# Attention with an RMS norm on q and k, then a token mixer and an MLP: batch 0's first loads, warming products, the cast of V and four fillers are rearranged

## The chip, the cores and the metric

The kernel runs on one core of one Trainium2 chip. The metric is the device time of one execution, in microseconds (us). Four runs of the kernel before gave 580.72, 579.29, 584.65 and 579.07; their median is 580.01. The engines are called PE (TensorE), DVE (VectorE), ACT (ScalarE), POOL (GpSimd) and SP (SyncE, which here only issues transfers).

## The reference

```
q, k, v: (8 batches, 12 heads, 448 tokens, 64), float32
q_n = rmsnorm(q, g_q);  k_n = rmsnorm(k, g_k)         # over the 64
attn = softmax(q_n k_n^T / 8);  o = attn v
x = o, heads side by side: (8, 448, 768)
u = x + (U V applied along the 448 tokens)            # rank 32
out = u + relu(u w_ch1) w_ch2                         # 768 -> 3072 -> 768
```

## The kernel before

**Tiles and stages.** A batch's 12 heads are three groups t of four heads, and each group is two pairs p of two heads. The 448 tokens lie as 112 partitions by 4. For a group, `load` and `load_v` fetch k, q and v (L187, L201); `squares` and `reduce` (L217, L227) give sums of squares, `rsqrt` (L234) makes two ScalarE instructions of them (Ln and Exp). For a pair, `scale` (L239) multiplies k and then q by the norm on DVE, from two SBUF inputs; `transposes` (L250) turns the eight pieces on PE and takes them out of PSUM with a multiply by the gain `gg` for q (L258) and a copy for k (L259). `scores` and `expo` (L267, L277) make exponentials of 112 x 896, `values` (L281) multiplies them with v and divides. Then the mixing with U and V and the MLP follow. From batch 1 on, attention is woven into the MLP of the batch before by weights (`weave`), so PE always has dense matmuls at hand.

**The head.** Batch 0 has no MLP to hide in. `head` (L591) writes its order by hand: loads first, then set-up, warming products, and the norm of group 0 in halves (A: heads 0 and 1, Bh: heads 2 and 3), then 24 slots. Slot n runs exponential n, then the pieces that `at(n, ...)` put on it in the order of writing, then the scores n + 2. After the slots, mixing and the first MLP columns (`first`, L724) follow, and the dense loop `mlp` (L482).

**Fillers and warming.** `heat(n)` (L755) issues n products of 128 x 512 on a zeroed tile into a PSUM buffer; nobody reads it. Its buffer is one of three of the pool `ps_mm` (tag "mm"), which `transposes`, `setup_u`, the mixing steps and every second `values` of batch 0 also take in turn; a new user waits until the one three before it has been read out. `heat(NWARM)` (L604) runs ahead of the first gain product.

**Queues.** Each engine executes its instructions in the order of writing. SP issues the loads of the head one after another: k and q of group 0 in halves (k, q, k, q), then groups 1 and 2, U and V, v of groups 0 to 2, group 3 (L594 to L602). ScalarE's queue issues only the two small gain loads (L135), after it has loaded its table (L121). POOL does squares of group 1's k and of groups 2 and 3, the casts of v (`cast_v`, L212), the two partial copies of V (L156, L157) and issues the weight loads. `yield_port` (L718) makes POOL wait for a scaling on DVE.

**The parts that the change touches.** `setup_v` (L154) casts V from float32 to bf16 in another order of its columns and makes two shifted copies; it stands in slot 11. `gain` (L137) multiplies the product of the two gains (formed at L607) with a one on PE and copies it to `gg`; its copy L141 stands on DVE ahead of the evacuation of the first transposes. The loads' line is

```
nc.sync.dma_start(qks[t, s][:, h:h + n], (k, q)[s][b, h0 + h:h0 + h + n]...)   # L198
```

Of the kernel before, what the change touches and what calls it, by code (L numbers as in the profile page):

```python
# [12 lines left out]
AF = mybir.ActivationFunctionType  # L13
# [4 lines left out]
def kernel(  # L18
# [13 lines left out]
    nc = tc.nc  # L32
# [7 lines left out]
    NJ = 4  # L40
# [43 lines left out]
    V4 = consts.tile([P, S], BF16, name="V4")  # L84
    Vsh = consts.tile([P, 2, P], BF16, name="Vsh")
    gg = consts.tile([P, 1], FP32, name="gg")
    grow = consts.tile([1, 2, 2, D], FP32, name="grow")
    one = consts.tile([1, 1], FP32, name="one")
    eps = consts.tile([SP, 1], FP32, name="eps")
    NWARM, NH = 16, 2  # L90
    FA, FM, NPE, FA0 = (0.74, 0.77), 0.09, 14, 0.66
    flat = Tw.rearrange("p f c n -> p (f c n)")
    lent = [0]
# [1 line left out]
    def lend(p, shape, dtype):  # L95

        n = 1
        for d in shape:
            n *= d
        n *= 2 if dtype == FP32 else 1  # L100
        a = flat[0:p, lent[0]:lent[0] + n]
        lent[0] += (n + 15) // 16 * 16
        a = a.bitcast(FP32) if dtype == FP32 else a
        names = "abcd"[:len(shape)]
        return a if len(shape) == 1 else a.rearrange(
            f"p ({' '.join(names)}) -> p {' '.join(names)}", **dict(zip(names, shape)))
# [30 lines left out]
    def gain():  # L137

        pg = ps_mm.tile([P, 1], FP32, tag="mm")
        nc.tensor.matmul(pg, grow[:, 0].rearrange("o a d -> o (a d)"), one, start=True, stop=True)  # L140
        nc.vector.tensor_copy(gg, pg)  # L141
# [4 lines left out]
    Vf = lend(P, [S], FP32)  # L146
# [3 lines left out]
    def load_mix():  # L150
        nc.sync.dma_start(Uf, moe_U.rearrange("(p j) r -> p (j r)", j=NJ))
        nc.sync.dma_start(Vf, moe_V.rearrange("r s -> () r s").to_broadcast([4, rank, S]))

    def setup_v():  # L154
        nc.scalar.activation(V4.rearrange("r (j p) -> r j p", j=NJ), Vf.rearrange("r (p j) -> r j p", j=NJ), AF.Copy)
        nc.gpsimd.tensor_copy(Vsh[:, 0, 0:64], V4[:, 384:448])  # L156
        nc.gpsimd.tensor_copy(Vsh[:, 1, 64:128], V4[:, 0:64])  # L157

# [26 lines left out]
    qks, vts, sqs, rstds, qkns, qkTs, scs, x3_of = {}, {}, {}, {}, {}, {}, {}, {}  # L185

    def load(t, parts=1, ss=(0, 1)):  # L187
        b, h0, n = t // 3, (t % 3) * HG, HG // parts
        for s in ss:
            if t in (2, 3):  # L190
                qks[t, s] = spare[0:SP, t - 2, s]
            elif (t, s) in ((1, 1), (5, 1)):
                qks[t, s] = k1
            else:
                qks[t, s] = loads.tile([SP, HG, NJ * D], FP32, tag="qk", name="qk", bufs=3)
        for h in range(0, HG, n):
            for s in ss:
                nc.sync.dma_start(qks[t, s][:, h:h + n],  # L198
                                  (k, q)[s][b, h0 + h:h0 + h + n].rearrange("h (p j) d -> p h (j d)", j=NJ))

    def load_v(t):  # L201
# [25 lines left out]
    def reduce(t, hs=ALL, ss=(0, 1)):  # L227
        if t not in rstds:
            rstds[t] = norm.tile([SP, 2, HG, NJ], FP32, tag="rstd", name="rstd", bufs=3)
        for s in ss:  # L230
            nc.vector.tensor_reduce(rstds[t][:, s, hs].rearrange("p h j -> p (h j)"),  # L231
                                    sqs[t, s][:, hs].rearrange("p h (j d) -> p (h j) d", d=D), AX, OP.add)
# [6 lines left out]
    def scale(t, pr):  # L239
        rstd, qkn = rstds[t], norm.tile([SP, 2, NJ, 2, D], BF16, tag="qkn", name="qkn")  # L240
        qkns[2 * t + pr] = qkn
        hp = slice(2 * pr, 2 * pr + 2)
        for s in range(2):
            nc.vector.tensor_tensor(  # L244
                qkn[:, s].rearrange("p j h d -> p h j d"),
                qks[t, s][:, hp].rearrange("p h (j d) -> p h j d", d=D),
                rstd[:, s, hp].rearrange("p h j -> p h j ()").to_broadcast([SP, 2, NJ, D]),
                OP.mult)

    def transposes(p):  # L250
        qkn = qkns[p].rearrange("p s j h d -> p (s j) (h d)")
        qkT = attn.tile([P, 2, S], BF16, tag="qkT")
        qkTs[p] = qkT
        if p < NPE:
            pt = ps_mm.tile([P, 2, S], BF16, tag="mm")
            for i in range(2 * NJ):
                nc.tensor.transpose(pt.rearrange("d s (j p) -> d (s j) p", j=NJ)[:, i, :], qkn[:, i, :], ident[:SP, :SP])  # L257
            nc.vector.tensor_scalar(qkT[:, 1], pt[:, 1], gg, None, OP.mult)  # L258
            nc.vector.tensor_copy(qkT[:, 0], pt[:, 0])  # L259
        else:  # L260
            nc.sync.dma_start_transpose(qkT.rearrange("d s (j p) -> d (s j) p", j=NJ), qkn)

# [253 lines left out]
    def attention(b, extra={}):  # L516
# [14 lines left out]
        for p in range(b * 6, b * 6 + 6):  # L531
# [5 lines left out]
            if p + 1 < NP and (p + 1 >= NPE or not odd):  # L537
                add(.5, transposes, p + 1)
# [52 lines left out]
    def head():  # L591

        A, Bh = slice(0, 2), slice(2, 4)
        load(0, 2)  # L594
        load(1)
        load(2)
        load_mix()
        load_v(0)
        load_v(1)
        load_v(2)  # L600
        load(3)
        load_v(3)  # L602
        setup()
        heat(NWARM)  # L604
        squares(0, A)
        reduce(0, A)
        nc.vector.tensor_mul(grow[:, 0], grow[:, 0], grow[:, 1])  # L607
        squares(0, Bh, (0,))
        rsqrt(0, A)
        squares(0, Bh, (1,))  # L610
        reduce(0, Bh, (0,))
        scale(0, 0)
        gain()
        reduce(0, Bh, (1,))
        transposes(0)
        heat(3)
        squares(1, ALL, (0,), nc.gpsimd)
        rsqrt(0, Bh)
        scores(0, (0, 1))
        fill = {n: [] for n in range(24)}  # L620

        def at(n, fn, *args):
            fill[n].append(lambda: fn(*args))

        at(0, scale, 0, 1)
        at(0, reduce, 1, ALL, (0,))
        at(0, heat, 3)
        at(0, transposes, 1)
        at(1, heat, 3)
        at(1, squares, 1, ALL, (1,))  # L630
        at(1, reduce, 1, ALL, (1,))
        at(1, yield_port, 0, 1)
        at(1, squares, 2)
        at(1, load_w1, 0)
        at(2, heat, 2)
        at(3, rsqrt, 1)
        at(3, scale, 1, 0)
        at(3, yield_port, 1, 0)
        at(3, nc.gpsimd.tensor_copy, Uc, Uf)
        at(3, cast_v, 0)  # L640
        at(3, heat, NH)
        at(4, heat, 2)
        at(5, heat, 1)
        at(6, heat, 1)
        at(5, transposes, 2)
        at(5, scale, 1, 1)
        at(5, yield_port, 1, 1)
        at(6, cast_v, 1)
        at(6, load_w1, 1)
        at(7, setup_u, 0)  # L650
        at(7, reduce, 2, ALL, (0,))
        at(8, transposes, 3)
        at(8, reduce, 2, ALL, (1,))
        at(8, cast_v, 2)
        at(9, setup_u, 1)
        at(9, heat, 1)
        at(10, values, 0, 0)
        at(11, values, 0, 1)
        at(11, setup_v)
        at(11, rsqrt, 2)  # L660
        at(11, scale, 2, 0)
        at(12, mix_a, 0, 0)
        at(12, heat, 1)
        at(13, transposes, 4)
        at(13, scale, 2, 1)
        at(13, load, 4)
        at(13, load_v, 4)
        at(13, load_w1, 2)
        at(14, values, 1, 0)
        at(14, yield_port, 2, 1)  # L670
        at(14, squares, 3)
        at(15, values, 1, 1)
        at(16, transposes, 5)
        at(16, load, 5)
        at(16, load_v, 5)
        at(16, load_w1, 3)
        at(16, cast_v, 3)
        at(16, mix_b, 0, 0)
        at(17, values, 2, 0)
        at(18, values, 2, 1)  # L680
        at(18, mix_a, 0, 1)
        at(19, values, 3, 0)
        at(19, mix_b, 0, 1)
        at(20, values, 3, 1)
        at(20, mix_a, 0, 2)
        at(21, values, 4, 0)
        at(21, mix_b, 0, 2)
        at(22, values, 4, 1)
        at(22, mix_a, 0, 3)
        at(23, mix_b, 0, 3)  # L690
        at(23, mix_a, 0, 4)
        for n in range(24):
            expo(*divmod(n, 4))
            for piece in fill[n]:
                piece()
            if n + 2 < 24:
                scores((n + 2) // 4, ((n + 2) % 4,))
        first(0, range(0, 3), True)
        values(5, 0)
        values(5, 1)  # L700
        mix_b(0, 4)
        first(0, (3,), False)
        first(1, range(0, 4), True)
        mix_a(0, 5)
        first(0, (4,), False)
        first(1, (4,), False)
        mix_b(0, 5)
        reduce(3)
        rsqrt(3)
        first(0, (5,), False)  # L710
        first(1, (5,), False)
        scale(3, 0)
        scale(3, 1)
        squares(4, ALL, (0,))
# [91 lines left out]
```

## Time and profile before

| | us |
|---|---|
| median of four runs | 580.01 (579.07 to 584.65) |
| the profiled execution's own time | 581.62 |
| its span, first to last instruction | 579.8 |
| PE busy in it | 563.0 (97%) |
| DVE, ACT, POOL busy | 398.0, 280.1, 79.1 |
| first product on PE | 3.81 |
| first scores (L273) | 11.23 |
| last exponential of batch 0 (L278) ends | 40.20 |
| first column product of the MLP (L732) | 41.46 |

Times in a profile are counted from the first instruction of the span. In a timeline a line gives the start, the duration of the group, the engine, the line of the kernel, the operation with what it writes and reads, how many instructions of the kind stand together, and in brackets how long the engine had been idle and what released it. In a table of stretches, each engine has its busy time and the number of its instructions; then follow the mean granted PE clock (1.00 is full), the mean busy share of the 16 DMA engines and the rate.

### The profile page before, as it was taken

What the parts mean: (1) busy time and instruction counts of PE and PEld (TensorE: products, weight loads), DVE (VectorE), ACT (ScalarE), POOL (GpSimd) and SP (SyncE); (2) the same over time, 40 slices, a digit from 0 to 9 for tenths busy, and PEclk for the clock granted to TensorE, in tenths of its full rate; (3) what the DMA queues carried; (4) which work ended last, traced back from release to release, by engine and by line L of the source; (5) the groups of instructions that cost most, each with busy time, mean ns of one, the idle gap of its engine ahead of it and who ended that gap; (6) DMA issues with size and microseconds to landing.
All of it is one profiled execution on the core that took longest, in us unless ns stands there. A gap on an engine that the chain in (4) does not pass through costs nothing.

```text
span 579.8 us, 11362 instructions
## 1 busy us (share of the span) xinstructions
PE 563.0 (97%) x4613; PEld 306.5 (53%) x4613; DVE 398.0 (69%) x811; ACT 280.1 (48%) x413; POOL 79.1 (14%) x122
## 2 busy tenths in 40 slices
PE   6899999999999999999999999999999999999997
PEld 2365556544465555544456555544456555554464
DVE  5868987399975787747777498756767587453342
ACT  5855663167621876166651677236661386302200
POOL 4742421000020001000020001000002010000010
PEclk9999999999999999999999999999999999999999
DMA  9999998514463355635536354646245431040021
GB/s 208 242 239 237 218 176 169 120 47 98 112 167 85 84 125 118 150 87 112 128 82 130 83 129 112 152 112 125 62 86 162 100 97 33 29 110 0 1 55 54
DMA packets 103648, 67.22 MB, mean 116 GB/s; under 512 B 54716, under 2 KB 102060, under 8 KB 103596
## 3 DMA queue, kind: packets, MB, share of 16 engines
q1 hardware_dynamic: 93988, 56.77, 41.8%
q0 software_dynamic: 9376, 9.44, 9.9%
q8 instruction: 36, 0.59, 0.4%
q10 hardware_dynamic: 232, 0.30, 0.2%
q14 instruction: 16, 0.13, 0.1%
HBM read 52.19 MB, written 11.01 MB: 109 GB/s over the span
## 4 chain that ended last, share of the span: by engine, by line
PE 85%; DVE 8%; DMA 3%; ACT 1%; issue 1%; POOL 1%; DVEq 0%; POOLq 0%; ACTq 0%
PE ph L488 35%; PE pb L413 10%; PE o L299 7%; PE pe L413 7%; PE po L413 7%; PE sc L273 7%; PE pa L413 6%; DMA qkT<-qkn 2%; DVE qkn L244 2%; PE pu L337 2%; DVE rstd L231 1%; ACT E L278 1%; PE warm L759 1%; PE first L732 1%; PE pt L257 1%
## 5 line engine op out<-in xcount | busy, mean ns | idle before, releaser
L488 PE MATMUL ph<-u,w1b 128*128 128x512 bf16 (+1 forms) x1128 | 232.9, 354 | 0.3
L278 ACT ACTIVATE E<-sc 112x896 bf16<-112x896 f32 x184 | 159.9, 914 | 59.8 <-PE sc L273 58.2
L488 PEld LDWEIGHTS <-w1b 128*128 128x128 bf16 x1128 | 102.8, 98 | 108.6 <-issue 22.4
L413 PEld LDWEIGHTS <-hT 128*128 128x128 bf16 x1080 | 101.2, 98 | 71.5 <-issue 8.8
L491 ACT ACTIVATE hT<-ph 128x384 bf16<-128x384 f32 (+1 forms) x95 | 51.4, 543 | 136.2 <-PE ph L488 134.4
L493 DVE TENSOR_SCALAR hT<-ph 128x512 bf16<-128x512 f32 (+1 forms) x93 | 57.9, 622 | 53.2 <-PE ph L488 52.4
L299 PEld LDWEIGHTS <-E 112*128 112x128 bf16 x1472 | 59.2, 99 | 16.5 <-DVE xs L306 1.9
L299 PE MATMUL o<-va,E 112*128 112x65 bf16 x1440 | 61.8, 195 | 0.8 <-DVE xs L306 0.8
L244 DVE TENSOR_TENSOR qkn<-qk,rstd 112x512 bf16<-112x512 f32 x84 | 56.9, 715 | 7.8 <-ACT rstd L237 3.9
L273 PE MATMUL sc<-qkT 64*128 64x448 bf16 x384 | 56.1, 358 | 3.1 <-ACT E L278 1.1
L720 POOL COPY scratch<-qkn 1x1 bf16<-1x1 bf16 x44 | 11.8, 268 | 306.8 <-DVE qkn L244 301.0
L413 PE MATMUL po<-w2b,hT 128*128 128x384 bf16 x288 | 52.5, 327 | 0.6 <-DVE hT L493 0.6
L231 DVE TENSOR_REDUCE rstd<-sq 112x16 f32<-112x1024 f32 x40 | 48.5, 1212 | 4.8 <-ACT sq L223 4.1
L413 PE MATMUL pa<-w2b,hT 128*128 128x384 bf16 x264 | 49.5, 326 | 0.0
L413 PE MATMUL pb<-Tw,hT 128*128 128x384 bf16 x264 | 48.1, 327 | 0.0
L223 ACT ACTIVATE sq<-qk 112x1024 f32<-112x1024 f32 x36 | 38.2, 1062 | 2.3 <-issue 1.1
L303 DVE TENSOR_TENSOR x<-o,rec 128x192 bf16<-128x192 f32 x96 | 34.3, 357 | 3.7
L448 POOL TENSOR_TENSOR o<-o,x 128x384 f32<-128x384 f32 x11 | 12.6, 1145 | 161.1 <-DVE o L447 161.1
L302 DVE RECIPROCAL rec<-o 128x4 f32<-128x4 f32 x96 | 17.0, 177 | 23.9 <-PE o L299 23.7
L273 PEld LDWEIGHTS <-qkT 64*128 64x128 bf16 x384 | 12.5, 94 | 35.3 <-issue 30.7
L428 ACT ACTIVATE pb<-pa 128x384 f32<-128x384 f32 x11 | 5.2, 475 | 50.3 <-PE pa L413 50.3
L339 DVE TENSOR_TENSOR x<-pu,x 128x768 bf16<-128x768 f32 (+1 forms) x27 | 23.3, 865 | 7.2 <-PE pu L337 7.0
(106 smaller groups left out, 450.5 us busy)
## 6 DMA issues: line engine op xcount, KB each, us to landing
qk<-in_k_dram SPq DMA_DIRECT2D x21, 448.0 KB, 6.2
vt<-in_v_dram SPq DMA_DIRECT2D x20, 448.0 KB, 5.0
qk<-in_q_dram SPq DMA_DIRECT2D x19, 448.0 KB, 3.9
w2b<-in_moe_w_ch_dram POOLq DMA_DIRECT2D x6, 768.0 KB, 11.4
w1b<-in_moe_w_ch_dram POOLq DMA_DIRECT2D x2, 1536.0 KB, 21.5
out_dram<-o SPq DMA_DIRECT2D x15, 168.0 KB, 2.7
out_dram<-o SPq DMA_DIRECT2D x16, 144.0 KB, 2.1
out_dram<-o SPq DMA_DIRECT2D x15, 120.0 KB, 2.5
```

What stands on the lines that cost most here:

```text
L223: nc.scalar.activation(sqs[t, s][:, hs], qks[t, s][:, hs], AF.Square)
L231: nc.vector.tensor_reduce(rstds[t][:, s, hs].rearrange("p h j -> p (h j)"), sqs[t, s][:, hs].rearrange("p h (j d) -> p (h j) d", d=D), AX, ...
L244: nc.vector.tensor_tensor(qkn[:, s].rearrange("p j h d -> p h j d"), qks[t, s][:, hp].rearrange("p h (j d) -> p h j d", d=D), rstd[:, s, h ...
L273: nc.tensor.matmul(sc[:, hh, 0:S], kT[pp, kc * SP:kc * SP + P], qT[pp, :], start=True, stop=True)
L278: nc.scalar.activation(E_of(p)[:, :, PAD + kc * S:PAD + (kc + 1) * S], scs.pop((p, kc))[0:SP, :, 0:S], AF.Exp, scale=float(D) ** 0.5)
L299: nc.tensor.matmul(o[:, i, :], E[:, hh, c:c + P], va[:, hl, kc, :], start=(kc == 0), stop=(kc == NJ - 1))
L303: nc.vector.tensor_tensor(x3[:, :, d0:d0 + D], o[:, t0:t0 + 3, 0:D], rec[:, t0:t0 + 3].rearrange("p c -> p c ()").to_broadcast([P, 3, D]), ...
L339: nc.vector.tensor_add(xv, pu[rows, 0:n, 0:HALF], xv)
L413: nc.tensor.matmul(ps, lhs[:, c, :], rhs[:, c, :], start=first and c == 0, stop=last and c == NC - 1, skip_group_check=again)
L488: nc.tensor.matmul(ph, w1b[:, dc, hc * P:(hc + 1) * P], u[:, dc, :], start=(dc == 0), stop=(dc == KD - 1))
L491: nc.scalar.activation(hT[:, hc, 0:n], ph, AF.Relu)
L493: nc.vector.tensor_relu(hT[:, hc, 0:n], ph)
```

## The change

Six edits, all for batch 0 but one. The first half of group 0's q is issued from ScalarE's queue, as that queue's first instruction, ahead of the table load; the other loads stay on SP. The first warming has 12 products instead of 16. V is cast by POOL. The evacuation of transposes copies k ahead of multiplying q, in all pairs that PE transposes (14). The product of the gains (L607) moves behind the first scaling, and the reduction of q's second half (L614) behind the first pair's transposes. Slots 10, 11, 14 and 15 get one filler each, written ahead of the values of their slots.

```
-    NWARM, NH = 16, 2
+    NWARM, NH = 12, 2
...
     def setup_v():
-        nc.scalar.activation(V4.rearrange("r (j p) -> r j p", j=NJ), Vf.rearrange("r (p j) -> r j p", j=NJ), AF.Copy)
+        nc.gpsimd.tensor_copy(V4.rearrange("r (j p) -> r j p", j=NJ), Vf.rearrange("r (p j) -> r j p", j=NJ))
...
-                nc.sync.dma_start(qks[t, s][:, h:h + n],
+                (nc.scalar if (t, s, h) == (0, 1, 0) else nc.sync).dma_start(qks[t, s][:, h:h + n],
...
+            nc.vector.tensor_copy(qkT[:, 0], pt[:, 0])
             nc.vector.tensor_scalar(qkT[:, 1], pt[:, 1], gg, None, OP.mult)
-            nc.vector.tensor_copy(qkT[:, 0], pt[:, 0])
...
         reduce(0, A)
-        nc.vector.tensor_mul(grow[:, 0], grow[:, 0], grow[:, 1])
         squares(0, Bh, (0,))
         rsqrt(0, A)
         squares(0, Bh, (1,))
         reduce(0, Bh, (0,))
         scale(0, 0)
+        nc.vector.tensor_mul(grow[:, 0], grow[:, 0], grow[:, 1])
         gain()
+        transposes(0)
         reduce(0, Bh, (1,))
-        transposes(0)
         heat(3)
...
         at(9, heat, 1)
+        at(10, heat, 1)
+        at(11, heat, 1)
+        at(14, heat, 1)
+        at(15, heat, 1)
         at(10, values, 0, 0)
```

More of the change, by code (lines that the diff above doesn't have):

```diff
@@ L89 @@
     eps = consts.tile([SP, 1], FP32, name="eps")
-    NWARM, NH = 16, 2
+    NWARM, NH = 12, 2
     FA, FM, NPE, FA0 = (0.74, 0.77), 0.09, 14, 0.66
@@ L154, in setup_v @@
     def setup_v():
-        nc.scalar.activation(V4.rearrange("r (j p) -> r j p", j=NJ), Vf.rearrange("r (p j) -> r j p", j=NJ), AF.Copy)
+        nc.gpsimd.tensor_copy(V4.rearrange("r (j p) -> r j p", j=NJ), Vf.rearrange("r (p j) -> r j p", j=NJ))
         nc.gpsimd.tensor_copy(Vsh[:, 0, 0:64], V4[:, 384:448])
@@ L197, in load @@
             for s in ss:
-                nc.sync.dma_start(qks[t, s][:, h:h + n],
+                (nc.scalar if (t, s, h) == (0, 1, 0) else nc.sync).dma_start(qks[t, s][:, h:h + n],
                                   (k, q)[s][b, h0 + h:h0 + h + n].rearrange("h (p j) d -> p h (j d)", j=NJ))
@@ L257, in transposes @@
                 nc.tensor.transpose(pt.rearrange("d s (j p) -> d (s j) p", j=NJ)[:, i, :], qkn[:, i, :], ident[:SP, :SP])
+            nc.vector.tensor_copy(qkT[:, 0], pt[:, 0])
             nc.vector.tensor_scalar(qkT[:, 1], pt[:, 1], gg, None, OP.mult)
-            nc.vector.tensor_copy(qkT[:, 0], pt[:, 0])
         else:
@@ L606, in head @@
         reduce(0, A)
-        nc.vector.tensor_mul(grow[:, 0], grow[:, 0], grow[:, 1])
         squares(0, Bh, (0,))
@@ L612, in head @@
         scale(0, 0)
+        nc.vector.tensor_mul(grow[:, 0], grow[:, 0], grow[:, 1])
         gain()
+        transposes(0)
         reduce(0, Bh, (1,))
-        transposes(0)
         heat(3)
@@ L656, in head @@
         at(9, heat, 1)
+        at(10, heat, 1)
+        at(11, heat, 1)
+        at(14, heat, 1)
+        at(15, heat, 1)
         at(10, values, 0, 0)
```

## The prediction

> **What bounds the kernel now.** I read the page first. TensorE sets the time, and only what moves its work can change the end:
>
> ```profile
> PE 563.0 (97%) x4613; PEld 306.5 (53%) x4613; DVE 398.0 (69%) x811; ACT 280.1 (48%) x413; POOL 79.1 (14%) x122
> ```
>
> PE is idle for 579.8 - 563.0 = 16.8 us in all, 3.81 of it before its first product. The diff touches the first 32 us (the head), so its worth is how much earlier the head hands over to the dense matmuls behind it (from 41 us on). I then read the timelines of the head, engine by engine. PE, start and duration first, in brackets the idle time before and its releaser:
>
> ```profile
> 3.81 5.61 PE L759 MATMUL warm<-xs 128*128 128x512 bf16 x16 [3.81 <-POOL xs L130]
> ...
> 11.23 0.55 PE L273 MATMUL sc<-qkT 64*128 64x448 bf16 x4 [0.35 <-DVE qkT L259]
> ...
> 12.69 0.37 PE L257 MATMUL pt<-ident,qkn 112*128 112x112 bf16 x4 [0.15 <-DVE qkn L244]
> ```
>
> The 16 warming products hold PE until 9.4, though VectorE has the first scaled pair ready at 8.53. But the next thing PE needs, the second pair's transposes at 12.69, waits for VectorE's scaling (L244). VectorE in turn:
>
> ```profile
> 11.14 2.10 DVE L244 TENSOR_TENSOR qkn<-qk,rstd 112x512 bf16<-112x512 f32 x2
> ...
> 16.80 1.60 DVE L244 TENSOR_TENSOR qkn<-qk,rstd 112x512 bf16<-112x512 f32 x1 [0.65 <-ACT rstd L237]
> ```
>
> One such scaling takes 0.68 when alone. Here two take 2.10 and one 1.60, and each ends about 0.55 after a GpSimd instruction that overlaps it:
>
> ```profile
> 10.20 1.89 POOL L225 TENSOR_TENSOR w2b<-qk 112x1024 f32<-112x1024 f32 x1 [5.64 <-DMA qk<-in_k_dram]
> ...
> 14.11 3.74 POOL L225 TENSOR_TENSOR w2b<-hT 112x1024 f32<-112x1024 f32 x2 [0.63 <-DMA hT<-in_k_dram]
> ...
> 25.75 1.04 POOL L213 CAST Tw<-hT 112x1024 bf16<-112x1024 f32 x1 [0.20 <-DMA hT<-in_v_dram]
> ```
>
> So up to 28 us the head is paced by: a transfer lands, GpSimd runs, VectorE waits for it, PE waits for VectorE. The third meeting is the scaling of group 2 (CAST until 26.79, VectorE):
>
> ```profile
> 25.95 2.02 DVE L244 TENSOR_TENSOR qkn<-hT,rstd 112x512 bf16<-112x512 f32 x2
> ```
>
> ScalarE, the engine that loses the cast of V (L155), waits for transfers early; its cast stands where PE waits for VectorE:
>
> ```profile
> 5.98 0.63 ACT L223 ACTIVATE w2b<-qk 112x512 f32<-112x512 f32 x1 [0.76 <-DMA qk<-in_k_dram]
> ...
> 23.91 1.02 ACT L155 ACTIVATE V<-Tw 128x448 bf16<-128x448 f32 x1
> ```
>
> Last, PE from 26 us on, and its clock by stretches (busy, count, granted clock, DMA share, GB/s):
>
> ```profile
> 25.95 0.24 PE L357 MATMUL pm<-x,Ub 128*32 128x128 bf16 x3 [1.07 <-DVE x L303]
> ...
> 28.81 1.06 PE L299 MATMUL o<-va,E 112*128 112x65 bf16 x16
> ```
>
> ```profile
> 24.83:28.24 3.41, 1.59 (x17) 1.00 1.16 249
> 28.24:31.65 3.41, 3.41 (x42) 0.52 1.19 254
> ...
> 574.37:577.78 3.41, 1.63 (x11) 1.00 0.46 133
> ```
>
> Sixteen value products take 1.06 at 28.81 and 0.68 at 32.90: after a stretch with PE busy for 47%, it ran 3.41 us at half clock. It is the only such stretch after the warm-up. The chain of waits has PE back to back in it.
>
> **What the Trainium skill says.** "TensorE: Matmul & The Clock Gate", Part 1: the array's clock is halved after an idle window of about 3.4 us, restored after a busy one, and the windows run free of the kernel. The trace agrees: warm products start 427 ns apart until 7.6 and 216 from 8.0, and the slow stretch lasts 3.41. "SBUF — State Buffer", SBUF: two separate sides: GpSimd and a VectorE operation with two SBUF inputs take a shared port for a whole instruction. The rows above agree. "DMA: Bandwidth & Descriptors", Queues, rings and completion order: SP and ACT have one ring each on the same 16 engines, taken in turn. No run here shows that yet; the DMA share is 0.9 or more for most of the time from 2 us.
>
> **The change part by part.**
>
> *q's first half on ScalarE's queue.* SP issues k at 0.74 and q at 1.18; now q goes at about 0.74 too and every later SP issue moves up by 0.49. The table load and the two small gain loads on ScalarE move back by about 0.5; their users come later (4 us, 8 us). The bytes share the same engines, so k's first half lands later (seen at 3.73; estimate 4.3), q's about as before (4.60), and the gating third piece (seen at 5.98) up to 0.49 earlier. What counts is the load behind GpSimd's squares at 10.20, and the two behind 14.11. The DMA engines were not full at 1.75 to 2.25 (170 GB/s against some 260 after) nor around 5.25 (135). Filling the first hole is worth about 0.2 us of bytes, both about 0.5. Bounds: -0.7 to +0.2 (a slowed k); I take -0.3, since only the first hole surely closes. It passes through 12.09 and 17.85, where VectorE waits.
>
> *12 warming products, gain multiply moved, qB's reduction behind the evacuation.* The four dropped ran at 216 ns: PE is free at 9.35 - 0.86 = 8.49. The gain multiply (0.27) follows the scaling, done at about 8.1 to 8.5, so the gain product starts at about 8.5 and first scores follow some 1.0 us before 11.23. The reduction moves from 9.84 to about 10.1, the second rsqrt from 10.55 to about 10.8, the second scaling from 11.14 to about 11.4. It still has to wait for GpSimd until 12.09, and PE's scores 2 and 3 are queued behind its transposes. Worth: 0, both ways, as long as the scaling is ready before 12.09 (0.7 spare); without that cover, +0.3. The copy/multiply swap at L258 (14 times) costs nothing: scores need both halves.
>
> *V's cast on GpSimd.* ScalarE gets 1.02 back at 23.91, but its next instruction (rsqrt of group 2) waits for VectorE's reduction until 24.62 and its exponentials wait for PE at 28.92 (1.06 idle): worth 0. On GpSimd, casts of 1024 and 128 columns take 1.04 and 0.28, so 448 take about 0.55. It is queued behind the CAST of 25.75 and ahead of the two Vsh copies and w1's third load, which have slack. It comes in between the two scalings of 25.95, where the first Vsh copy got in before; the second scaling would then end 0.4 later, and with it group 2's transposes. Bounds 0 to +0.55; I take +0.4.
>
> *Fillers.* Each takes a buffer of the three of `ps_mm`. Slot 10's waits for the evacuation of pair 3's transposes (VectorE, 23.49), slot 11's for the copy of Ub (24.81): the values behind them slip from 22.99 and 23.89 to about 23.7 and 25.0. This is hidden: VectorE is busy until 24.74 and then blocked by the CAST until 26.79. So 0 (bound +0.4), but PE's work is spread into the idle stretch: in 24.83 to 28.24 about 0.43 of filler and 0.6 of values join the 1.59, some 75%. Slots 14 and 15 lie where PE is back to back: 2 x 0.22 = +0.44, no cover; at half clock 2 x 0.43 = +0.86.
>
> *The clock.* 75% stayed at full clock elsewhere (38.48 to 41.89: 2.59 of 3.41), even 48% did at the end. At full clock the stretch from 28.33 (four scores groups of two, 32 values, transposes) needs about 2.9 instead of 4.4: -1.5.
>
> Sum against the profiled execution: span 579.8 - 0.3 + 0.4 + 0.44 - 1.5 = 578.8. That execution took 581.62 (1.8 around the span), 1.6 above the median of the runs, 580.01. Of the four, two lie at 579.07 and 579.29 and one at 580.72, 1.5 higher: I read the slow stretch as absent in two and present in one. From 579.2 without it: -0.3 + 0.4 + 0.44 = 579.7; a run with it would come from 580.7 to the same place. The cast may find VectorE already done and then costs less than the 0.4, so I take half of it off: 579.5.
>
> **The rivals.**
> 1. *Early start passes through* (0.2): the landings gain the full 0.7 and GpSimd, VectorE and PE all move; the cast meets no scaling. 579.2 - 0.7 + 0.44 = 578.9, down to 578.0 if the fillers find idle PE. Against it: the saturated transfers.
> 2. *Fillers don't hold the clock, and end slower* (0.15): the slow stretch stays, and slots 14 and 15 pay 0.86 in it: 580.7 + 0.86 + 0.4 - 0.3 = 581.7, or about 580.9 as a median with runs without it. It decides where the busy share of the window stays below about 47%.
> 3. *Nothing moves* (0.15): landings and cast worth 0, fillers find slack: 580.0.
> The forecast, net of small terms with the clock held, has 0.5; its own range is 579.0 to 580.2.
>
> **Range and chances.** From rival 1's full gain to rival 2's median: 577.9 to 581.0. A measurement of this kernel tells about 1% (5.8 us) from no change; PE's whole idle time after its first product is 13 us and the edits reach perhaps 3 of it, so no case here gets there: within 1% 0.96, 0.02 on either side for what I don't see.
>
> **What would show it.** First scores near 10.2 but pair 1's transposes still near 12.5; GpSimd's squares of group 1 at 9.9 (landing gain) or 10.2 (none); the second scaling of 25.95 ending after the V cast; fillers of slots 10 and 11 starting late; value products at 28 to 31 us at 0.6 to 0.7 for sixteen. I am wrong if transposes of pair 1 start before 12, if the clock falls again, or if the time leaves the range because something after 41 us moved.

## The result, and the profile after

Two figures are kept apart in what follows: a kernel's median and its ratio to the kernel before, and the mean over the executions in which PE's clock stayed full (mean granted clock of 0.9985 or more; "at full clock" below), because a stretch of 3.41 us at half clock, which comes in some executions of nearly every kernel here, costs about 1.6 us by itself. One stretch lowers the mean clock of an execution by 0.003, so 0.995 or less means two or more of them: the profiled executions with one have 0.997, those with two 0.994 and 0.993. (Executions at 0.998, nine of all, fall between and are counted as not full.)

| | kernel before | kernel after |
|---|---|---|
| median of all executions beside each other | 581.24 (63) | 580.64 (44) |
| ratio, 95% interval | | 0.9991 [0.9979, 1.0002] |
| executions not at full clock | 83 of 185 | 20 of 58 |
| of these at 0.995 or less (two stretches or more) | 47 | 2 |
| mean at full clock, one standard error | 580.30 ± 0.08 | 580.22 ± 0.12 |
| mean over all of these executions | 581.29 ± 0.11 | 580.86 ± 0.17 |
| profiled execution's own time, span | 581.62, 579.8 | 582.02, 580.2 |

The 185 are the executions of the kernel before beside the experiments (67, 51 and 67 on three chips, with means at full clock of 580.35, 580.25 and 580.30), the 58 are the 44 of the result and a second group of 14. The result beside each other shows no difference: the interval of the ratio holds 1. The forecast was 579.5 against 580.01, 0.5 less; the medians differ by 0.6. The level was taken 1.2 too low, since the four runs known then had a median of 580.01 and the 63 have 581.24. At full clock 0.08 ± 0.15 is left of the change; over all executions the mean falls by 0.43 ± 0.20, because fewer have two stretches or more. The question is why six edits in the head, some of them worth 0.7 us or more as the experiments show, come to nothing at full clock. First the page's engine line of the kernel after:

```profile
PE 562.5 (97%) x4613; PEld 306.5 (53%) x4613; DVE 396.4 (68%) x811; ACT 279.4 (48%) x412; POOL 80.3 (14%) x123
```

PE is still the bound: idle for 580.2 - 562.5 = 17.7 us, 3.81 of it before its first product. One instruction has moved from ACT to POOL (V's cast). The timeline of PE after, at the same places as before:

```profile
3.81 4.37 PE L763 MATMUL warm<-xs 128*128 128x512 bf16 x12 [3.81 <-POOL xs L130]
...
10.43 0.55 PE L273 MATMUL sc<-qkT 64*128 64x448 bf16 x4 [0.19 <-DVE qkT L259]
...
12.35 0.37 PE L257 MATMUL pt<-ident,qkn 112*128 112x112 bf16 x4 [0.60 <-DVE qkn L244]
```

The first scores come 0.80 earlier than before (11.23), pair 1's transposes only 0.34 earlier (12.69), and PE now waits 0.60 for them where it waited 0.15. VectorE, the scalings of the second half of group 0 and of group 2:

```profile
11.60 1.29 DVE L244 TENSOR_TENSOR qkn<-qk,rstd 112x512 bf16<-112x512 f32 x2 [0.62 <-ACT rstd L237]
...
24.92 1.75 DVE L244 TENSOR_TENSOR qkn<-hT,rstd 112x512 bf16<-112x512 f32 x2
```

And GpSimd, with what it waited for:

```profile
9.28 1.89 POOL L225 TENSOR_TENSOR w2b<-qk 112x1024 f32<-112x1024 f32 x1 [4.72 <-DMA qk<-in_k_dram]
...
23.51 1.04 POOL L213 CAST Tw<-hT 112x1024 bf16<-112x1024 f32 x1
24.49 0.98 POOL L155 CAST V<-Tw 128x448 bf16<-128x448 f32 x1
```

Three things are to be read. Group 1's k lands 0.92 earlier (9.28 against 10.20). GpSimd is therefore done at 11.17, and the scaling at 11.60 no longer waits for it: it has its full speed (1.29 for two) but stands idle for 0.62 on the rsqrt, which comes late. And V's cast lies ahead of the first scaling of group 2, and overlaps it.

The head hands over earlier: the first MLP column product is at 40.62 instead of 41.46. Yet this execution took 0.4 longer than the one profiled before. From 30 to 208 us PE is 0.7 to 0.9 ahead, and then it loses 0.47 at 208 us, 0.15 at 359, 0.28 at 367 and 0.18 at 517. The second profile of the unchanged kernel, against the first, loses 0.3 to 0.45 at each of the same four places. The time from the first hidden-layer product (L488) to the end, work that the change does not touch but for the order of two evacuations, was 531.77 and 532.58 in two profiles of the kernel before, 532.97 and 532.93 after, and 531.7 to 533.9 in fourteen profiles of all kernels. One pair of profiles thus can't settle a change of half a microsecond at the end; it shows what happens in the head, and the runs show what it is worth.

### The profile page after: what moved, and what is told of

It reads as the page before. It is cut to its first block, busy times and chain, and to the rows that moved or that the text cites. A ratio compares the mean times of both kernels' runs of the same rounds, so it can differ in the third digit from the quotient of the medians.

```text
span 580.2 us, 11359 instructions
## 1 busy us (share of the span) xinstructions
PE 562.5 (97%) x4613; PEld 306.5 (53%) x4613; DVE 396.4 (68%) x811; ACT 279.4 (48%) x412; POOL 80.3 (14%) x123
## 4 chain that ended last, share of the span: by engine, by line
PE 83%; DVE 7%; DMA 6%; ACT 2%; issue 1%; ACTq 0%; DVEq 0%
PE ph L488 34%; PE pb L413 11%; PE pe L413 7%; PE o L299 7%; PE pa L413 7%; PE sc L273 7%; PE po L413 7%; DMA qkT<-qkn 5%; DVE qkn L244 2%; PE pu L337 2%; DVE rstd L231 1%; ACT E L278 1%; DMA grow<-in_g_k_dram 1%; PE first L736 1%; PE pt L257 1%
## 5 line engine op out<-in xcount | busy, mean ns | idle before, releaser
L488 PE MATMUL ph<-u,w1b 128*128 128x512 bf16 (+1 forms) x1128 | 232.8, 353 | 0.6 <-DMA u<-x 0.2
L488 PEld LDWEIGHTS <-w1b 128*128 128x128 bf16 x1128 | 102.9, 98 | 108.9 <-issue 22.7
L244 DVE TENSOR_TENSOR qkn<-qk,rstd 112x512 bf16<-112x512 f32 x84 | 55.5, 698 | 8.4 <-ACT rstd L237 4.6
```

Source lines behind the costliest of these rows:

```text
L244: nc.vector.tensor_tensor(qkn[:, s].rearrange("p j h d -> p h j d"), qks[t, s][:, hp].rearrange("p h (j d) -> p h j d", d=D), rstd[:, s, h ...
L488: nc.tensor.matmul(ph, w1b[:, dc, hc * P:(hc + 1) * P], u[:, dc, :], start=(dc == 0), stop=(dc == KD - 1))
```

## The experiments

These were the theories at the start. *Landing:* two queues bring the data of group 1 sooner, and this passes to the end. *Cover gone:* the new order of VectorE, priced at nothing because GpSimd's squares hid it, now costs time because they end earlier. *GpSimd in the way:* V's cast delays group 2's scaling. *Fillers:* those in slots 14 and 15 are paid for in full. *Rival:* nothing in the head reaches the end. Differences below are between means at full clock, ± one standard error (the sorting by clock was made after the fact, and the kernels did not all run beside one another, so a difference of less than two errors is unresolved); the mean over all executions is given where it says something else; ratios are to the kernel before, run beside each, over all its comparable executions.

### The kernels before and after once more

Unchanged, to see what one profile can tell.

> The kernel before once more, unchanged. It gives a second profile of it and the scatter of a ratio that should be 1. Both theories expect 1.000 within about 0.002, and between a third and a half of its executions with a half-clock window. In a profile without such a window the first MLP column product should lie near 39.9 (41.46 less the 1.5 that the window is taken to cost); if it lies at 41 or more the window costs less than was predicted.

> The changed kernel once more, beside the others. Expected: about a third of the executions with a half-clock window, full-clock mean near 580.1, and in a profile at full clock a first MLP column product near 39.2; the landing gain (GpSimd's squares of group 1 near 9.0) present again, the second scaling again about 0.6 behind the end of those squares.

Before again: ratio 0.9995 [0.9979, 1.0011], mean at full clock 580.61 ± 0.17; the squares of group 1 start at 9.92, pair 1's transposes at 12.42, the column product is at 41.40, after two half-clock windows in a row (from 20.4). After again: 1.0000 [0.9985, 1.0015], mean at full clock 580.57 ± 0.23, squares at 8.92, second scaling at 11.53, 0.72 behind their end, column product at 40.74. The reading of the head holds in both; a profile of the kernel after at full clock was not obtained, since both have the half-clock stretch at 27.6. The same kernel in another group of executions thus differs by 0.36 ± 0.24 (before, on one chip) and 0.46 ± 0.27 (after): steps below 0.5 in what follows are weak.

### q's first half alone, and all but it

```
# e1: before, with only this line of after; e2: after, with this line as before
-                nc.sync.dma_start(qks[t, s][:, h:h + n],
+                (nc.scalar if (t, s, h) == (0, 1, 0) else nc.sync).dma_start(qks[t, s][:, h:h + n],
```

> The kernel before with one edit: the first half of q on ScalarE's queue. Theory L (landings): this edit alone gives the whole gain of the head. GpSimd's squares of group 1 start at 9.3 (before 10.20, changed kernel 9.28), and the first MLP column product (before 41.46) at about 40.2 without a half-clock window in the head or 0.9 earlier than before with one. Rival S (early start): the head's gain comes from fewer warming products and the new order on VectorE and PE; then the squares may start earlier but the column product stays within 0.3 of 41.46 when the clock window is alike. Time: L about 0.9 us below the kernel before, S none.

> The changed kernel with q's first half back on SP's queue. Theory L: GpSimd's squares of group 1 back near 10.2, pair 1's transposes near 12.6, and the fillers of slots 14 and 15 and the cast of V left as costs: the time is 0.3 to 0.9 us above the kernel before. Rival S: squares back at 10.2, but the column product still 0.5 or more ahead of the kernel before, time below it.

Alone it gives 0.9978 [0.9962, 0.9993], -0.66 ± 0.24 against before. Taken out of the change, it makes the rest slower: 1.0029 [1.0010, 1.0048], +1.24 ± 0.31 against after. Over all executions these are -0.99 ± 0.33 and +1.95 ± 0.43: with q back on SP, 6 of 22 executions have two stretches or more, against 2 of 58 after. In e1's profile the column product stands later than before, at 42.94. That execution has two half-clock stretches (12.9 and 30.0), and its head starts late, because VectorE waits for a gain load:

```profile
9.14 0.28 DVE L607 TENSOR_TENSOR grow<-grow 1x128 f32<-1x128 f32 x1 [2.76 <-DMA grow<-in_g_k_dram]
```

The first scaling starts at 9.95 instead of 7.25 and the first scores come at 14.17 instead of 11.23. This is a price of the edit: the two gain loads of 0.5 KB now stand behind q's 224 KB on ScalarE's queue. All five profiled kernels with q on that queue and the product of the gains in its old place (e1, e7, e9, e10, e11) wait for it, by 0.22 to 2.76; before and b0 don't, and none of the six with q on that queue and the product behind the first scaling does. So e1's profile says little on the handover, and the runs carry this verdict. e2's profile misses what was expected as well: pair 1's transposes at 12.19, and the column product at 40.31 in an execution without a half-clock stretch. The squares of group 1 start at 9.53 in e1 and at 9.59 in e2, which alone would show no difference. Over all profiles they start at 10.20, 9.92 and 9.59 with q on SP and from 8.19 to 9.93, mean 9.01, in eleven with q on ScalarE: a mean gain of 0.9 with a scatter about as large, which one profile can miss.

What the second queue does to the rate is seen in tables of stretches (SP's busy time, its count, the clock, the mean busy share of the DMA engines, GB/s). The kernel before:

```profile
1.75:2.75 1.00, 1.00 0.87 233
2.75:3.75 1.00, 1.00 1.01 285
3.75:4.75 1.00, 1.00 0.91 215
4.75:5.75 1.00, 1.00 0.89 185
```

and the kernel after:

```profile
1.75:2.75 1.00, 1.00 0.70 172
2.75:3.75 1.00, 1.00 1.10 379
3.75:4.75 1.00, 1.00 1.13 243
4.75:5.75 1.00, 1.00 1.08 252
```

In these 4 us, 1046 KB are moved instead of 918, but one pair of profiles says too much: b0 moves 1054 and e2 893. Over all profiles the three with q on SP have 224 to 263 GB/s in the 4 us (mean 239), the eleven others 239 to 270 (mean 256). Two things hold in every one: the early hole does not close (209 to 233 with q on SP, 93 to 205 otherwise), and the stretch from 2.75, which looked full, is faster (281 to 292, against 354 to 381). The mean gain of 17 GB/s is 68 KB, by estimate some 0.3 us of the 0.9; group 1's k is also issued 0.62 earlier (2.18 instead of 2.80). How the two share the gain was not separated.

### The new order on VectorE, and the number of warming products

```
# e7: after, with the old order
+        nc.vector.tensor_mul(grow[:, 0], grow[:, 0], grow[:, 1])   # behind reduce(0, A)
...
+        reduce(0, Bh, (1,))
         transposes(0)
...
# e6: after, with
+    NWARM, NH = 16, 2
```

(e7 has the evacuation's multiply and copy in their old order too.)

> The changed kernel with VectorE's old order: gain product ahead, the reduction of q's second half ahead of the first pair's evacuation, q's multiply ahead of k's copy. Theory W: the second scaling starts about 0.3 earlier, at 11.3 instead of 11.6, and with GpSimd's squares of group 1 now done at 11.2 it no longer waits for them, so pair 1's transposes and the column product come 0.2 to 0.4 earlier and the time is 0.3 lower. Rival S: the old order delays the first scores by about 0.5 and the time rises by that.

> The changed kernel with 16 warming products again. Theory W (hidden start): nothing after 13 us moves, since pair 1's transposes wait for VectorE's scaling and not for the first scores; time as the changed kernel within 0.3. Rival V (12 products are too few): with 16 fewer executions start cold after the warming, and the time falls by 0.5 or more. Rival S (early start pays): the time rises by about 0.5.

e7's ratio is 1.0006 [0.9983, 1.0029] with 8 of 14 executions not at full clock; at full clock it is 0.53 ± 0.44 below after. Its VectorE line shows what the order does:

```profile
10.42 1.34 DVE L244 TENSOR_TENSOR qkn<-qk,rstd 112x512 bf16<-112x512 f32 x2
```

The second scaling starts at 10.42 instead of 11.60, as soon as VectorE has taken out the first transposes and 0.2 before GpSimd's squares end (8.72 to 10.61), pair 1's transposes at 11.65 instead of 12.35, and the column product at 38.27 instead of 40.62. Of these 2.35, about 1.6 belong to the half-clock stretch that e7's profile lacks.

With 16 products, e6 is at 0.9991 [0.9974, 1.0008], and 0.67 ± 0.25 above after at full clock. First scores move from 10.43 to 11.23, the second scaling from 11.60 to 12.39, pair 1's transposes from 12.35 to 13.14: all by 0.79 or 0.80, close to the 0.86 of four products. In the new order the reduction of q's second half stands behind the evacuation of the first transposes, and these stand behind the warming products on PE: so the second norm waits for PE's warming. It did so in the old order too, by a shorter way: there it stands behind the copy of the gain product, which waited in the kernel before:

```profile
9.77 0.16 DVE L141 COPY gg<-pg 128x1 f32<-128x1 f32 x1 [1.24 <-PE pg L140]
```

### V's cast, and the fillers

```
# e5: after, with
+        nc.scalar.activation(V4.rearrange(...), Vf.rearrange(...), AF.Copy)
# e8: e5, and without
-        at(14, heat, 1)
-        at(15, heat, 1)
# e3: after, without all four fillers (slots 10, 11, 14, 15)
```

> The changed kernel with V cast by ScalarE as before. Theory P (port): the second scaling of group 2 no longer waits for GpSimd's cast, the two scalings take 1.3 to 1.4 instead of 1.75, and all of PE from slot 13 on is 0.3 to 0.4 earlier; time 0.3 lower than the changed kernel. Rival A (ScalarE was short): the exponentials of slots 12 to 14 come 0.5 to 1.0 later, PE's scores with them, time 0.3 or more higher.

> The changed kernel with V cast by ScalarE and fillers in slots 10 and 11 alone. Theory F: against the run with V on ScalarE and all four fillers the two products of 0.22 in slots 14 and 15 are gone from a stretch where PE is back to back: 0.44 less, and few executions with a half-clock window (at most 3 in 22), because slots 10 and 11 lie in the weak stretch. It would be the fastest version: about 1.0 below the kernel before at full clock, 1.3 in the median. Rival G: slots 14 and 15 guard a later stretch too, and the share with a window goes back to a third.

> The changed kernel without the four fillers. Theory F (fillers only cost): as many executions as with them, about a third, hold a half-clock window, and the time of those without one falls by 0.44, to some 0.9 below the kernel before. Rival C (fillers guard the clock): clearly more executions hold a half-clock window than the changed kernel's 15 of 44, and the median rises by 0.3 or more.

With V back on ScalarE the two scalings of group 2 take

```profile
25.54 1.28 DVE L244 TENSOR_TENSOR qkn<-hT,rstd 112x512 bf16<-112x512 f32 x2
```

against 1.75 after, where V's cast was in the way. That is not the cast's doing alone: they take 1.75 in e9 too, where V is on ScalarE, beside GpSimd's cast of v (L213, 23.18 to 24.22),

```profile
23.65 1.75 DVE L244 TENSOR_TENSOR qkn<-hT,rstd 112x512 bf16<-112x512 f32 x2
```

and 2.02 before. Over all profiles the pair takes 1.28 to 2.25 (mean 1.82) in the seven with V on GpSimd and 1.28 to 2.02 (mean 1.53) in the seven with V on ScalarE: what counts is which GpSimd instruction happens to lie there. In time nothing is left of it at full clock: after is 0.04 ± 0.19 below e5. Over all executions after is 0.44 ± 0.27 above e5, whose ratio is 0.9982 [0.9967, 0.9997]: only 1 of e5's 22 executions is not at full clock, against 20 of 58. That the cast brings the stretches is not shown; with the same edit, e9 and e11 have 7 of 22 each.

Without the fillers of slots 14 and 15 (e8) the ratio is 0.9978 [0.9963, 0.9993], and e5 stands 0.83 ± 0.23 above e8. In the profiles, the stretch from group 2's scaling to the column product is 13.88 in e5 and 13.44 in e8: 0.44, just the two products. Without all four (e3) the ratio is 0.9999 [0.9981, 1.0016], 0.13 ± 0.42 above after at full clock, with 7 of 14 executions not at full clock: too few executions to resolve it, and a miss for the theory that fillers cost what they last.

### q's load, 12 products and the fillers of slots 10 and 11 alone

```
# e9: before, with q on ScalarE's queue, and
-    NWARM, NH = 16, 2
+    NWARM, NH = 12, 2
...
+        at(10, heat, 1)
+        at(11, heat, 1)
# e10: e9 with 16 products; e11: e9 with V cast by GpSimd
```

> The kernel before with three edits only: q's first half on ScalarE's queue, 12 warming products, fillers in slots 10 and 11; VectorE's order and V's cast as before. Theory O (the new order eats the landing gain): the second scaling starts at about 10.5 instead of 11.6, pair 1's transposes at about 11.7, the first MLP column product near 38.3 to 38.6 in a profile at full clock; full-clock executions mean 579.0 or less, 1.2 or more below the kernel before, and 0.4 below the run with the new order, V on ScalarE and fillers in slots 10 and 11 (579.4). Rival (order is neutral): within 0.2 of that run.

> As the run with q on ScalarE's queue, 12 products and two fillers, but with 16 warming products. Theory O: with the landing 0.9 earlier the warming is on the path now: PE is held until about 9.4, the gain copy and with it VectorE's reduction and second scaling slip by 0.5 to 0.9, and the time is 0.4 to 0.8 higher. Rival (hidden start): no difference, since pair 1's transposes wait for the landing.

> As the run with q on ScalarE's queue, 12 products and two fillers, but with V cast by GpSimd. Theory P: the cast takes about 1.0 on GpSimd and blocks one of group 2's scalings for 0.4 to 0.7; the transposes of pair 4 come that much later; time 0.2 to 0.5 higher and more executions with a half-clock window. Rival: VectorE gets the scalings in ahead of the cast, no difference.

e9 has the lowest ratio and the lowest time at full clock: 0.9969 [0.9951, 0.9988], 578.99 ± 0.19. Over all executions e8, e9 and e10 are alike (579.70 ± 0.21, 579.78 ± 0.33, 579.79 ± 0.25). e9 differs from e8 only in the order on VectorE (with that of the evacuation's multiply and copy), and stands 0.45 ± 0.26 below it at full clock; with e7 against after, the same edit, the two together, weighted by their errors, give 0.47 ± 0.22. Its second scaling starts at 9.95, before GpSimd's squares end at 10.22:

```profile
9.95 1.42 DVE L244 TENSOR_TENSOR qkn<-qk,rstd 112x512 bf16<-112x512 f32 x2
```

e10 has 0.9970 [0.9957, 0.9983] by its ratio, since 1 of its 22 executions is not at full clock and 7 of e9's 22; at full clock it is 0.86 ± 0.32 above e9. So at full clock the warming products count in the old order as well. e10's profile can't show the place: its loads landed late (squares at 9.93), and VectorE waited for the gain load, as in e1:

```profile
8.93 0.28 DVE L607 TENSOR_TENSOR grow<-grow 1x128 f32<-1x128 f32 x1 [2.35 <-DMA grow<-in_g_k_dram]
```

e11 has 0.9976 [0.9961, 0.9991], 0.31 ± 0.31 above e9. Its cast of V takes 1.44, inside group 2's scalings of 2.25:

```profile
26.02 1.44 POOL L155 CAST V<-Tw 128x448 bf16<-128x448 f32 x1
```

The loss is seen in the trace and not resolved in time.

## Why the prediction was right, and where its steps were wrong

Seven of the kernels make a ladder from before to after, one edit a step (differences of means):

| step | from, to | predicted | at full clock | all executions |
|---|---|---|---|---|
| q's first half on ScalarE's queue | before, e1 | -0.3 | -0.66 ± 0.24 | -0.99 ± 0.33 |
| fillers in slots 10 and 11 | e1, e10 | 0 (-1.5 with the clock) | +0.20 ± 0.34 | -0.51 ± 0.40 |
| 12 products for 16 | e10, e9 | 0, with the next (+0.3 uncovered) | -0.86 ± 0.32 | -0.01 ± 0.42 |
| new order on VectorE | e9, e8 | 0, with the one before | +0.45 ± 0.26 | -0.08 ± 0.39 |
| fillers in slots 14 and 15 | e8, e5 | +0.44 | +0.83 ± 0.23 | +0.72 ± 0.30 |
| V's cast on GpSimd | e5, after | +0.4 | -0.04 ± 0.19 | +0.44 ± 0.27 |
| sum | before, after | | -0.08 ± 0.15 | -0.43 ± 0.20 |

The total was right with some luck. The prediction's terms make the kernel 0.3 to 0.5 slower at full clock and let the clock pay for it. At full clock, gains of 0.66 and 0.86 met a loss of 0.83, and one of 0.45 that is not resolved by itself. The rest, 0.35 over all executions, did come from the clock, as predicted, but not in the way predicted.

**q's queue: right place and sign, term too small.** Issue at 0.73, k's first half seen later (4.49 instead of 3.73), q's about as before, the third piece seen at 5.79 instead of 5.98: as predicted. The failed step is "only the first hole surely closes": that hole did not close, and the rate rose behind it (281 to 292 GB/s from 2.75 to 3.75 became 354 to 381). The small gain loads, whose users were to come later, became a wait of up to 2.76 in the kernels that leave the product of the gains where it was; in the kernel after, which moves it behind the first scaling, they did not. "DMA: Bandwidth & Descriptors", Queues, rings and completion order, on two rings served in turn, agrees with k's half being slowed (4.49 instead of 3.73); that the rate from 2.75 to 3.75 is higher with two queues at work is what these runs add.

**Warming and order: the cover was counted before the other edit moved it.** The prediction gave both together 0 "as long as the scaling is ready before 12.09 (0.7 spare)". But 12.09 is when GpSimd's squares end, and these wait for the load which the first edit speeds up. They ended at 11.17 and the scaling began at 11.60 instead of the expected 11.4: the spare was gone. At full clock the 12 products are then worth 0.67 ± 0.25 (e6) and 0.86 ± 0.32 (e10 and e9); that they were worth nothing before the landing moved was not tested. The new order costs 0.47 ± 0.22 over its two pairs of kernels. It mixes edits that pull apart: the product of the gains behind the first scaling spares the wait for the gain load, the reduction behind the first transposes delays the second scaling (11.60 against 10.42 in e7). A kernel with the first and without the second was not built, and may be better than e9.

**V's cast: seen, but elsewhere and longer.** In the profile it took 0.98, not 0.55, since the nearest row was taken by its columns alone: 1024 contiguous columns take 1.04 here, and these 448, which are read in another order, nearly as long. It came ahead of the first scaling of group 2, not between the two, and the pair took 1.75 instead of e5's 1.28, which is 0.47, near the 0.4; but 2.02 before, and the mean difference over all profiles is 0.29. "SBUF — State Buffer", SBUF: two separate sides, agrees: the cast and the scaling don't run at full speed together. At full clock e5 and e11 don't show this as time (-0.04 ± 0.19, +0.31 ± 0.31), and over all executions +0.44 ± 0.27 is not resolved: +0.4 is not confirmed. That ScalarE's freed 1.02 is worth nothing was right: its next instruction (L236, at 23.62) had waited 0.63 for VectorE's reduction.

**Fillers 10 and 11: wrong premise, small effect.** They were to wait for buffers until 23.7 and 25.0. They did not; in PE's timeline after, neither shows a wait, both start before the evacuation and the copy that were to hold them have ended (22.46 and 23.79), and the values follow at once:

```profile
21.96 0.39 PE L763 MATMUL warm<-xs 128*128 128x512 bf16 x1
22.18 0.67 PE L299 MATMUL o<-va,E 112*128 112x65 bf16 x16
...
23.09 0.39 PE L763 MATMUL warm<-xs 128*128 128x512 bf16 x1
```

So the rule that a filler takes its turn behind those readers is wrong here; which buffer it takes instead, the profile doesn't show. The values did not slip, and less of PE's work than assumed came into the idle stretch.

**Fillers 14 and 15: right in the trace, small by the runs.** 0.44 in the profiles of e5 and e8, 0.83 ± 0.23 by their executions; the half-clock price (0.86) doesn't explain it, since these are means at full clock. What makes up the rest is open.

**The clock: the step that failed.** "75% stayed at full clock elsewhere, even 48% did at the end" was to keep this stretch at full clock. PE after, by windows of 3.41 us (busy, count, clock, DMA share, GB/s):

```profile
20.75:24.16 3.41, 3.41 (x53) 1.00 1.15 241
24.16:27.57 3.41, 2.29 (x21) 1.00 1.17 245
27.57:30.98 3.41, 3.41 (x39) 0.50 1.18 247
```

The window has PE busy for 2.29 of 3.41, 67% and not 75% (55% in the second profile of after), and the next ran at half clock all the same. In fourteen profiles, the windows of the head with 60% or less (six of them) were all followed by half clock, this one of 67% was, and one of 64% (e11) and all of 69% to 73% were not. The 48% at the end of the kernel was no evidence for the head. "TensorE: Matmul & The Clock Gate", Part 1, agrees with windows that run free: in one trace they start on a grid of 3.413 us from the warm-up, and the warm-up itself comes anywhere from 6.7 to 9.8 us. So how the weak stretch lies in the windows differs from one execution to the next, and a profile shows one draw: 34% of executions after, against 45% before, are not at full clock. Over all executions the stretches cost 0.99 in the mean before (581.29 - 580.30) and 0.64 after (580.86 - 580.22), 0.35 less, where 1.5 had been counted for executions that have one. That is fewer executions with two stretches or more (47 of 185, 2 of 58), which the prediction did not think of; those with one are more frequent after (36 of 185, 18 of 58). The fillers aren't shown to bring it: with them in place and q's load back on SP (e2), it is 6 of 22 again, and without them (e3) 1 of 14. The price of a single stretch was about right: 1.6 after (581.85 against 580.22), 1.3 before (581.61 against 580.30), 1.5 predicted.

**The rivals.** Rival 1 (the early start passes through) had the right mechanism, but in the kernel after the new order stops it: pair 1's transposes at 12.35, and at 11.18 in e9, which is closest to the kernel that rival 1 describes. Rival 2 (the clock isn't held, and slots 14 and 15 pay) is right in its mechanism for the profiled executions, and the end isn't slower because rival 1's gain pays for it. Rival 3 (nothing moves) is near in the number at full clock for the wrong reason: much moved.

**What stays open.** Why 7 of 80 executions of e5, e6, e8 and e10 are not at full clock, and 35 of 94 of after, e7 and e9; and why executions with two stretches or more are rarer with q's load on ScalarE's queue. A count of products doesn't tell them apart: e5 and e8 have 12, e6 and e10 have 16. And why fillers that can be seen to cost 0.44 in slots 14 and 15 seem to cost 0.83 by the runs, while e3, without any of the four, does not show a gain.

Of e9's gain a part is given back later: its column product is 3.9 earlier than before (1.6 of that is the clock), and its span 1.8 shorter. In its profile PE waits 0.88 for VectorE's evacuation (L259) at 60.5, and 0.75 of the head start is lost by 63.7 us; the rest of its run, 533.1 from the first hidden-layer product, lies in the scatter of the other profiles, 531.7 to 533.2.

## What to carry to other kernels

When several edits are priced together, ask of each "hidden behind X" whether another of the edits moves X: here a faster load removed the cover under which a reordering and four warming products were priced at nothing. When a load is put at the head of another queue, look at what stood there: a load of 0.5 KB became a wait of up to 2.76. Don't put an instruction that only needs VectorE and ScalarE behind one that waits for PE, or the wait is inherited (the second norm behind the first transposes). And where an effect comes in a third or half of the executions, count it over executions before a profile that has it, or lacks it, is explained.

## What the runs showed of the hardware that was not expected

With one load of four moved from SP's queue to ScalarE's, the 16 DMA engines moved 354 to 381 GB/s from 2.75 to 3.75 us in eleven profiles, against 281 to 292 in the three with one queue, where the kernel before had read as busy at 1.01: a busy share near 1 with one queue did not mean that the rate was at its limit. A load of 0.5 KB issued at 2.45 on ScalarE's queue behind that 224 KB was waited for until 6.39 to 9.14 in five profiles. A cast of 128 x 448 from float32 on GpSimd that reads in another order of columns took 0.98, and 1.44 beside a scaling on VectorE; 112 x 1024 in order took 1.04. And a window with PE busy for 67% was followed by half clock, while one with 64% was not, so the busy share of a window by this profile doesn't decide alone. The meeting of GpSimd and VectorE cost either side: group 2's pair of scalings took 1.75 to 2.25 in eight profiles and 1.28 in six, and in one of these six (e7) GpSimd's cast of v beside it took 1.88 instead of 1.04.
